# Decode attention over two KV caches: K and V in rows of 160 tokens, five heads to a group, in place of rows of 128 tokens and two heads

## The chip, the cores and the metric

One NeuronCore of a Trainium2 chip runs the whole program. The metric is the device time of one execution in microseconds (us). Engines are named as in the profile: PE (TensorE), PEld (its weight loads), DVE (VectorE), ACT (ScalarE), POOL (GpSimd), SP (SyncE, which issues nearly all transfers). The sequencer of an engine is the part that branches, computes addresses, waits for semaphores and hands instructions on; its own steps carry a `q` in the profile (PEldq, SPq).

## The reference

Two independent blocks A and B are computed and their outputs laid side by side. Each is one decode step of attention with batch 2, 32 heads, one query token and a cache of 8192 tokens, head size 192, model width 640, all bf16:

```python
q = (x @ wq).reshape(B, 1, 32, 192).transpose(0, 2, 1, 3)
scores = jnp.einsum("bhqd,bhkd->bhqk", q, k_cache) * (192 ** -0.5)
p = softmax(scores, axis=-1)
o = jnp.einsum("bhqk,bhkd->bhqd", p, v_cache)
return o.transpose(0, 2, 1, 3).reshape(B, 1, 32 * 192) @ wo
```

K and V of both blocks are 805 MB; with wq and wo it is 837 MB, each byte read once.

## The kernel before, in words

**Units.** Seen flat, a cache is 2 x 32 heads of 8192 tokens of 192 numbers. One load takes two heads as 128 rows of 128 tokens (`T = 128`, 49152 B a row): partitions 0 to 63 hold the first head, 64 to 127 the second. There are 32 such units to a block, 64 in all (`NP`); each has one load of K and one of V (6144 KB each).

**Ring.** `rings` has three slots of 61440 B a partition. K and V loads go round them: a load may be issued when the load two before it has landed (`ks`, `vs`) and when the slot's last user is done (`pv` for V's matmuls, `su` for the scores' matmuls). This is written out in `next_k` and `next_v` on SP. The same slots hold wq at the start and wo at the end.

**One unit.** The loop over `t` on each engine:

- PE, `make_q` (L322): one matmul with a selector spreads the two heads' queries over the partitions in PSUM; ACT (L272, L273) copies them to `qt`.
- DVE (L241): K is multiplied in place by the query, in four pieces of 32 tokens (128 x 6144 elements each).
- PE (L370): the 192 products of a token are added up in part: 12 matmuls with the identity add 16-wide pieces into `scps` (one PSUM bank for a piece of 32 tokens). The loop over `h` makes two turns of 24 matmuls.
- DVE (L246): reduces the last 16 to one score; L250 and L251 take each partition's maximum; POOL (L191) takes it over partitions; ACT (L296) scales it.
- ACT (L302): exp with the sum of each row (`rs`) into `pb`.
- PE (L385): PV. 64 matmuls of 384 columns, two tokens each, in four turns of a loop over `g` with 16 matmuls (`PG = 16`). Every turn tests the semaphore `vh`.
- `closing` on DVE and `gather` on ACT add the two halves and divide by the row sum; `put` on PE (L327) places the result in `oall`, four matmuls a unit.

PE's order in turn `t` of its loop (from L356) is: `make_q(t + 1)`, scores of unit `t`, `put`, PV of unit `t - 1`. So the scores of a unit stand ahead of the PV of the unit before.

**Ends.** At the start PE multiplies x by wq of both blocks (L411, six turns of ten matmuls a block) as wq lands. At the end wo of block A, the last V in two halves, and wo of block B in pieces (`PIECES`) are loaded; `rows` (L339) multiplies by wo.

Of the kernel before, what the change touches and what calls it, by code (L numbers as in the profile page):

```python
# [5 lines left out]
ALU = mybir.AluOpType  # L6
# [3 lines left out]
F32 = mybir.dt.float32  # L10
def build_kernel(nc, blocks, out):
# [5 lines left out]
    PB = Hn // 2  # L17
    UB = B * PB
    NP = NBLK * UB
    T = 128  # L20
    TQ = T // 4
    QW = TQ * Dh
# [4 lines left out]
    RW = T * Dh  # L27
    SW = DC * N
    QC = 512
    NQP = N // (2 * QC)  # L30
    NH2 = D // 2
    WR = N // 128
    PW = 34
    PG = 16
    PQ = T // 2 // PG
    CUTS = [48]
    PIECES = [24, 15, 6, 2, 1]

    with ExitStack() as es:
# [4 lines left out]
        sc = sb("sc", [128, T], F32)  # L44
        qt = sb("qt", [128, Dh], BF16)
        mp = sb("mp", [128, 2], F32)
        mg = sb("mg", [128, 2], F32)
        nb = sb("nb", [128, 1], F32)
        rs = sb("rs", [128, PW], F32)
        rc = sb("rc", [2, 1], F32)  # L50
        oodd = sb("oodd", [2, Dh], F32)
        on = sb("on", [2, Dh], BF16)
        xr = sb("xr", [4, D], BF16)
        xT = sb("xT", [128, DC, 4], BF16)
        ident = sb("ident", [128, 128], BF16)
        place = sb("place", [2, 264], BF16)
        ones = sb("ones", [128, 1], F32)
        oallS = sb("oallS", [128, WR, B], BF16)
        actd = sb("actd", [128, 2], F32)
        warm = sb("warm", [128, 2], F32)  # L60
        sb("pad", [128, 1648], BF16)
        rings = sb("rings", [128, 3 * SW], BF16)
        qrow = sb("qrow", [36, N], BF16)
        pb = sb("pb", [128, T // 2, PW], BF16)
        sel = sb("sel", [36, NBLK * B, 128], BF16)
        out_sb = [sb(f"out_sb{k}", [PW, NH2], BF16) for k in range(NBLK)]
# [4 lines left out]
        oall = ps("oall", [128, 2, 512], F32)  # L71
        outps = qps
        scflat = scps[:].rearrange("p k n -> p (k n)")
        oflat = oall[:].rearrange("p k n -> p (k n)")

        Z = {n: sem(n) for n in ("held", "wq", "wq0", "wq1", "xs", "k0", "ks", "vs", "vh", "os", "init", "dv", "xp", "xt",
                                 "pr", "qe", "qk", "qtd", "mu", "su", "re", "mx", "ar", "nbd", "ex", "pv", "od", "dd", "on",
                                 "pl", "oa", "ca", "oe", "wa0")}
# [7 lines left out]
        def flat(name, blk):  # L86
            return blocks[blk][name].rearrange("b h s d -> (b h s d)").rearrange("(u f) -> u f", f=RW)

        def k_slot(eng, t):
            return eng.snap(((t * 2 + 2 - ((t + (NP - 1)) >> 6)) % 3) * SW)  # L90

        def program_sync(eng):
# [5 lines left out]
            def load(name, blk, row, at, sem):  # L98
                src = flat(name, blk)
                src = src[row:row + 128, :] if isinstance(row, int) else src[bass.ds(row, 128), :]  # L100
                dst = rings[:, at:at + RW] if isinstance(at, int) else rings[:, bass.ds(at, RW)]
                eng.dma_start(dst, src).then_inc(Z[sem], 16)  # L102

            load("k", 0, 0, 2 * SW, "k0")
            eng.wait_ge(Z["pr"], NQP)
            load("k", 0, 128, 0, "ks")
            eng.wait_ge(Z["pr"], 2 * NQP)
            load("v", 0, 0, SW, "vs")
            eng.wait_ge(Z["su"], 2)

            def next_k(u, row, blk, at, wait_k, wait_p):
                hold(eng, "ks", wait_k)
                hold(eng, "pv", wait_p)
                load("k", blk, row, at, "ks")

            def next_v(u, row, blk, at, wait_v, wait_s):
                hold(eng, "vs", wait_v)
                hold(eng, "su", wait_s)
                load("v", blk, row, at, "vs")

            def step(t, u0, blk_v, blk_k):
                if isinstance(t, int):
                    u = u0
                    next_k(u, (u + 1) % UB * 128, blk_k, ((2 * u + 3) % 3) * SW, 16 * u + 16, PQ * (u + 1))
                    next_v(u, u % UB * 128, blk_v, ((2 * u + 4) % 3) * SW, 16 * u, 2 * u + 2)
                else:
                    u = eng.snap(t + u0)
                    r = eng.snap((u * 2) % 3)
                    rk, rv = eng.snap(t * 128 + (u0 + 1) % UB * 128), eng.snap(t * 128 + u0 % UB * 128)
                    next_k(u, rk, blk_k, eng.snap(r * SW), eng.snap(u * 16 + 16), eng.snap(u * PQ + PQ))  # L130
                    next_v(u, rv, blk_v, eng.snap(((r + 1) % 3) * SW), eng.snap(u * 16), eng.snap(u * 2 + 2))

            with eng.Fori(0, UB - 2) as t:
                step(t, 1, 0, 0)
            step(0, UB - 1, 0, 1)
            with eng.Fori(0, UB - 1) as t:
                step(t, UB, 1, 1)
            eng.wait_ge(Z["pv"], PQ * NP)
            for blk in range(NBLK):
                w = blocks[blk]["wo"].rearrange("(p r) n -> p (r n)", r=WR)  # L140
                if not blk:
                    r0 = 0
                    for k, n in enumerate(CUTS):
                        eng.dma_start(rings[:, r0 * D:(r0 + n) * D], w[:, r0 * D:(r0 + n) * D]).then_inc(Z[f"wa{k}"], 16)
                        r0 += n
                    eng.wait_ge(Z["su"], 2 * NP)
                    src = flat("v", 1)[(UB - 1) * 128:UB * 128, :]
                    for g in range(2):
                        a, e = g * RW // 2, (g + 1) * RW // 2
                        eng.dma_start(rings[:, SW + a:SW + e], src[:, a:e]).then_inc(vq[g], 16)  # L150
                else:
                    r0 = 0
                    for k, n in enumerate(PIECES):
                        eng.wait_ge(Z["ca"], k + 1)
                        eng.dma_start(rings[:, r0 * D:(r0 + n) * D], w[:, r0 * D:(r0 + n) * D]).then_inc(ws[k], 16)
                        r0 += n
# [8 lines left out]
        def program_pool(eng):  # L165
            eng.memset(warm[:], 0.0).then_inc(Z["init"], 1)
            eng.wait_ge(Z["init"], 1)
            eng.partition_all_reduce(warm[:, 1:2], warm[:, 0:1], 128, bass.bass_isa.ReduceOp.max)
            eng.memset(ident[:], 1.0).then_inc(Z["init"], 1)
            eng.wait_ge(Z["init"], 2)  # L170
            eng.affine_select(out=ident[:], in_=ident[:], compare_op=ALU.is_equal, fill=0.0, base=0,
                              pattern=[[-1, 128]], channel_multiplier=1).then_inc(Z["init"], 1)
            eng.memset(sel[:], 1.0).then_inc(Z["init"], 1)
            eng.wait_ge(Z["init"], 4)
            for k in range(NBLK * B):
                eng.affine_select(out=sel[:, k, :], in_=sel[:, k, :], compare_op=ALU.is_equal, fill=0.0,
                                  base=-(34 * (k // B) + k % B), pattern=[[0, 128]], channel_multiplier=1)
            eng.memset(place[:], 1.0).then_inc(Z["init"], 1)
            eng.wait_ge(Z["init"], 5)
            eng.affine_select(out=place[:], in_=place[:], compare_op=ALU.is_equal, fill=0.0, base=-128,  # L180
                              pattern=[[1, 264]], channel_multiplier=-4)
            eng.memset(ones[:], 1.0)
            eng.memset(rs[:], 0.0)
            eng.memset(pb[:], 0.0)
            eng.memset(mp[:], -3.0e38).then_inc(Z["init"], 1)
# [3 lines left out]
            with eng.Fori(0, NP) as t:  # L189
                hold(eng, "mx", eng.snap(t + 1))  # L190
                eng.partition_all_reduce(mg[:], mp[:], 128, bass.bass_isa.ReduceOp.max).then_inc(Z["ar"], 1)  # L191
            k = 0
            for i, n in enumerate(CUTS):
                eng.wait_ge(Z[f"wa{i}"], 16)
                while k < len(PIECES) and sum(PIECES[:k + 1]) <= sum(CUTS[:i + 1]):
                    eng.sem_inc(ws[k], 16)
                    k += 1
            eng.wait_ge(vq[0], 16)
            eng.sem_inc(Z["vs"], 16)
            eng.wait_ge(vq[1], 16)  # L200
            eng.sem_inc(Z["vh"], 2)

        def spread(eng, blk):
            eng.wait_ge(Z["pl"], (blk + 1) * UB + 3)
            dst = oallS[:].rearrange("p r b -> p b r")
            src = oall[:, 1 - blk, :].rearrange("p (b r) -> p b r", b=B)[:, ::-1, 0:WR]
            return eng.activation(dst, src, ACTF.Identity) if blk else eng.tensor_copy(dst, src)

        INIT = 6

        def program_vector(eng):
            eng.memset(qrow[:], 0.0).then_inc(Z["dv"], 1)  # L212
            eng.memset(on[:], 0.0)
            eng.memset(oodd[:], 0.0)
            eng.memset(ops[0:PW, 0:2 * Dh], 0.0)
            eng.memset(oall[:], 0.0)
            eng.memset(ops[0:2, 448:449], 1.0).then_inc(Z["dv"], 1)
            eng.sem_inc(Z["on"], 1)
# [3 lines left out]
            def closing(c):  # L222
                eng.wait_ge(Z["pv"], PQ * c if isinstance(c, int) else eng.snap(c * PQ))
                eng.reciprocal(rc[:], ops[0:2, 448:449]).then_inc(Z["dd"], 1)  # L224
                eng.wait_ge(Z["od"], c)
# [31 lines left out]
        def program_scalar(eng):  # L257
# [17 lines left out]
            for blk in range(NBLK):  # L275
# [4 lines left out]
                if not blk:  # L280
                    eng.wait_ge(Z["qk"], 1)
                    make_qt()
# [198 lines left out]
```

## Time and profile before

| what | value |
|---|---|
| median of 3 runs | 1935.44 us (1935.39 to 1935.62) |
| profiled execution, first to last instruction (span) | 1934.3 us |
| busy share PE / PEld / DVE / ACT / POOL | 81% / 38% / 56% / 10% / 1% |
| moved by DMA | 836.78 MB, 433 GB/s over the span |
| mean granted PE clock | 0.965 of full speed |

The profiled execution has no time of its own beside its span; the runs are 1.1 us longer than it. How to read the rows that follow: a row of groups gives line, engine, operation, output and input with their shapes and the count, then busy time and mean ns of one, then how long the engine stood idle before them and what ended that. A row of the timeline gives start, length, engine, line, operation, count, and in brackets the idle time before it with what ended it; "issue" there means that nothing but the engine's own sequencer was waited for. A row of windows gives for a stretch the busy time and number of instructions on PE, PEld, DVE, ACT and POOL, then the granted clock, the DMA engines' busy share and GB/s.

### The profile page before, as it was taken

How to read it: one execution, taken by the hardware profiler on the slowest of the kernel's cores; microseconds unless marked ns; L12 is line 12 of the kernel's file. 1: busy time of each engine (PE TensorE's matmuls, PEld its weight loads, DVE VectorE, ACT ScalarE, POOL GpSimd, SP SyncE). 2: the span in 40 equal slices, each digit the busy share in tenths (PEclk: the TensorE clock that was granted, in tenths of full speed). 3: DMA queues.
4: the chain of work that ended last, by engine and by line, in shares of the span. 5: the costliest groups of instructions: out<-in, count | busy, mean ns of one | idle time of the engine just before them, and what ended most of it. 6: DMA issues, size and time to landing. Idle time of an engine off the chain costs nothing.

```text
span 1934.3 us, 31141 instructions
## 1 busy us (share of the span) xinstructions
PE 1558.2 (81%) x7939; PEld 743.0 (38%) x7939; DVE 1075.6 (56%) x717; ACT 186.5 (10%) x598; POOL 27.9 (1%) x83
## 2 busy tenths in 40 slices
PE   5787888887888887888887888887888888888887
PEld 1343333333333333333333333333433333433434
DVE  0665565565565565565565565565565565565560
ACT  2110010010010010010010010010010010010010
POOL 1000000000000000000000000000000000000000
PEclk9899999999999999999999999999999999999999
DMA  9999999999999999999999999999999999999999
GB/s 421 425 439 439 423 439 439 425 437 439 430 432 439 431 431 439 433 429 439 435 427 439 437 425 439 437 425 439 437 425 439 439 425 437 439 430 432 439 435 394
DMA packets 19896, 836.78 MB, mean 433 GB/s; under 512 B 2220, under 2 KB 2360, under 8 KB 2744
## 3 DMA queue, kind: packets, MB, share of 16 engines
q1 hardware_dynamic: 19880, 836.78, 100.0%
q10 hardware_dynamic: 16, 0.01, 0.0%
HBM read 836.77 MB, written 0.01 MB: 433 GB/s over the span
## 4 chain that ended last, share of the span: by engine, by line
DMA 44%; PE 32%; DVE 10%; issue 10%; another core or an unknown queue 2%; DVEq 1%; SPq 0%; ACT 0%; POOLq 0%
DMA rings<-in_B_k_cache_dram 22%; DMA rings<-in_A_k_cache_dram 19%; PE ops L385 18%; PE scps L370 12%; DVE rings L241 10%; DMA rings<-in_A_wo_dram 2%; DMA rings<-in_B_wo_dram 1%; DVEq L241 1%; PE oall L327 0%; PE qps L339 0%; PE ops L379 0%; SPq L102 0%; DVE qrow L212 0%; DVE sc L246 0%
## 5 line engine op out<-in xcount | busy, mean ns | idle before, releaser
L241 DVE TENSOR_TENSOR rings<-rings,qt 128x6144 bf16 x256 | 842.5, 3353 | 722.9 <-DMA rings<-in_B_k_cache_dram 351.0
L385 PE MATMUL ops<-rings,pb 128*34 x4096 | 712.9, 327 | 166.9 <-issue 166.9
L370 PE MATMUL scps<-rings,ident 128*128 x3072 | 749.0, 403 | 105.5 <-DVE rings L241 102.6
L385 PEld LDWEIGHTS ops<-rings,pb 128*34 x4096 | 381.3, 93 | 483.0 <-issue 233.5
L370 PEld LDWEIGHTS scps<-rings,ident 128*128 128x128 bf16 x3072 | 314.5, 102 | 524.0 <-issue 249.6
L246 DVE TENSOR_REDUCE sc<-scps 128x64 f32<-128x1024 f32 x128 | 155.5, 1215 | 81.4 <-PE scps L370 81.4
L286 ACT ACTIVATE oodd<-ops 2x192 f32<-2x192 f32 x65 | 20.9, 321 | 731.4 <-PE ops L385 731.4
L272 ACT ACTIVATE qt<-qps 64x192 bf16<-64x192 f32 x65 | 21.0, 323 | 650.1 <-DVE rings L241 649.6
L302 ACT ACTIVATE pb<-sc,nb 64x128 bf16<-64x128 f32 x128 | 82.4, 644 | 2.6
L322 PE MATMUL qps<-qrow,sel 36*128 (+1 forms) x66 | 21.8, 331 | 72.4 <-issue 69.6
L296 ACT ACTIVATE nb<-mg 64x1 f32<-64x1 f32 x128 | 25.7, 201 | 302.8 <-POOL mg L191 302.1
L191 POOL PARTITION_ALL_REDUCE mg<-mp x64 | 22.7, 354 | 1856.8 <-DVE mp L251 1856.8
L322 PEld LDWEIGHTS qps<-qrow,sel 36*128 (+1 forms) x66 | 6.1, 93 | 94.0 <-issue 94.0
L302 ACT ACTIVATION_READ_ACCUMULATOR pb<-sc,nb 64x1 f32 x128 | 39.2, 306 | 0.0
L411 PE MATMUL scps<-rings,xT 128*4 x120 | 29.4, 410 | 6.3 <-POOLq L188 6.3
L224 DVE RECIPROCAL rc<-ops 2x1 f32<-2x1 f32 x66 | 9.8, 149 | 34.5 <-PE ops L385 34.5
L327 PEld LDWEIGHTS oall<-on,place 2*128 x260 | 12.5, 92 | 29.7 <-issue 29.2
L226 DVE TENSOR_TENSOR oodd<-ops,oodd 2x192 f32<-2x192 f32 x66 | 21.5, 326 | 0.4 <-ACT oodd L286 0.4
L229 DVE TENSOR_SCALAR on<-oodd,rc 2x192 bf16<-2x192 f32 x66 | 20.3, 307 | 2.3
L273 ACT ACTIVATE qt<-qps 64x192 bf16<-64x192 f32 x65 | 21.1, 325 | 0.8
L327 PE MATMUL oall<-on,place 2*128 2x48 bf16 x260 | 19.6, 183 | 1.9 <-DVE on L229 1.7
L411 PEld LDWEIGHTS scps<-rings,xT 128*4 128x4 bf16 x120 | 10.7, 89 | 24.2 <-issue 12.2
(38 smaller groups left out, 109.9 us busy)
## 6 DMA issues: line engine op xcount, KB each, us to landing
rings<-in_A_k_cache_dram SPq DMA_DIRECT2D x32, 6144.0 KB, 26.8
rings<-in_A_v_cache_dram SPq DMA_DIRECT2D x32, 6144.0 KB, 26.5
rings<-in_B_k_cache_dram SPq DMA_DIRECT2D x32, 6144.0 KB, 26.7
rings<-in_B_v_cache_dram SPq DMA_DIRECT2D x31, 6144.0 KB, 26.6
rings<-in_B_wq_dram SPq DMA_DIRECT2D x1, 7680.0 KB, 37.9
rings<-in_A_wo_dram SPq DMA_DIRECT2D x1, 7680.0 KB, 30.7
rings<-in_A_wq_dram SPq DMA_DIRECT2D x1, 7296.0 KB, 20.2
rings<-in_B_v_cache_dram SPq DMA_DIRECT2D x2, 3072.0 KB, 26.8
```

The lines of the kernel that those rows point to most:

```text
L191: eng.partition_all_reduce(mg[:], mp[:], 128, bass.bass_isa.ReduceOp.max).then_inc(Z["ar"], 1)
L226: eng.tensor_tensor(oodd[:], ops[0:2, 0:Dh], oodd[:], ALU.add).then_inc(Z["dd"], 1)
L241: eng.tensor_tensor(k3, k3, q3, ALU.mult).then_inc(Z["mu"], 1)
L246: eng.tensor_reduce(sc[:, h * 2 * TQ:(h + 1) * 2 * TQ], scps[:, 2 * h:2 * h + 2, :].rearrange("p k (t g) -> p (k t) g", g=DG), AXL.X, ALU. ...
L273: eng.activation(qt[64:128, :], qps[64:128, Dh:2 * Dh], ACTF.Identity).then_inc(Z["qtd"], 1)
L296: ins = eng.activation(nb[p0:p0 + 64, :], mg[p0:p0 + 64, h:h + 1], ACTF.Identity, scale=-scale)
L302: ins = eng.activation(pb[p0:p0 + 64, :, h::32], sc[p0:p0 + 64, :].rearrange("p (j a) -> p j a", a=2), ACTF.Exp, bias=nb[p0:p0 + 64, :], s ...
L322: eng.matmul(qps[:, 0:2 * Dh], sel[:].rearrange("p s m -> p (s m)")[:, bass.ds(k, 128)], qrow[:, bass.ds(c, 2 * Dh)], start=True, stop=Tru ...
L327: ins = eng.matmul(oflat[:, bass.ds(sec, WR)], place[:, bass.ds(at - a, 128)], on[:, a * WR:(a + 1) * WR], start=False, stop=False, skip_g ...
L370: ins = eng.matmul(dst, ident[:], src[:, :, 0:DG], start=(j == 0), stop=(j == NJ - 1))
L385: ins = eng.matmul(ops[0:PW, 0:2 * Dh], pbflat[:, bass.ds(aj + j * PW, PW)], rings[:, bass.ds(vj + j * (2 * Dh), 2 * Dh)], start=False, st ...
L411: ins = eng.matmul(scflat[0:4, bass.ds(to + h * QC, QC)], xT[:, c, :], rings[:, bass.ds(at + (c * N + h * QC), QC)], start=(c == 0), stop= ...
```

## The change

Rows become 160 tokens (five chunks of 32, 61440 B a partition), so that one load fills a whole slot (7680 KB). 8192 is no multiple of 160: two loads of 128 rows hold five heads (40960 tokens), and a partition can hold the end of one head and the start of the next. Which chunk of a partition belongs to which of the five heads is told by masks: `MK` spreads the right query over each partition (six matmuls, for up to three different queries of a load), `MN` adds -1e38 to the maxima and biases of chunks that aren't the head's, so that their exponentials are zero. A block is 12 groups of five heads and one group of four heads with rows of 128 tokens (`kind(t)`); there are 26 groups (`NG`).

- SP: four loads a group through the same three slots, in the order K_a, K_b, V_a, V_b, two semaphores (`la`, `lb`) in turn. The last V_b comes in pieces of three chunks and one.
- PE: order in turn `t` is `queries(t)`, `put`, PV of group `t - 1` (both V loads), scores of group `t` (both K loads). PV has 80 matmuls a load in ten turns of eight (`PG = 8`); `queries` has a loop of five matmuls, a copy by ACT and six matmuls into `scps`; `put` has eight matmuls; scores run in turns of 12 matmuls.
- DVE: five multiplies of K_a, one of K_b, reduction of K_a's scores, four multiplies of K_b, closing, reduction of K_b's scores, then maxima by chunk, masks, maxima by head and biases.
- ACT: copies of the queries, then 18 exponentials a group (three spans of a row by three heads, for each load).
- POOL: builds the masks at the start, and between two maxima passes on the landing of both V loads (`vs`).
- Start: the queries of a block come in twelve turns of five matmuls, and all of them ahead of the first group.

The diff, cut to the lines that run in the loops:

```diff
-        T = 128
+        TC = 32; CW = TC * Dh; NCH = 5; SCH = 4; T = NCH * TC; NS = 5
-        PG = 16
-        PQ = T // 2 // PG
+        PG = 8
+        LATE = 3
+        SPANS = [[(0, 1), (1, 2), (2, 5)], [(0, 3), (3, 4), (4, 5)]]
-        scps = ps("scps", [128, 4, 512], F32)
+        scps = ps("scps", [128, NCH, 512], F32)
...
 # SP
+            def step(g, row, blk, nch, unit):
+                hold(eng, "la", val(g * 32))
+                hold(eng, "su", val(g * (2 * NCH)))
+                load("k", blk, row, nch, s0, "la")
+                hold(eng, "lb", val(g * 32))
+                hold(eng, "pv", val(g * 2 + 1))
+                load("k", blk, row1, nch, s1, "lb")
+                if not isinstance(g, int) or g < NG - 1:
+                    hold(eng, "la", val(g * 32 + 16))
+                    hold(eng, "pv", val(g * 2 + 2))
+                    load("v", blk, row, nch, s2, "la")
+                    hold(eng, "lb", val(g * 32 + 16))
+                    hold(eng, "su", val(g * (2 * NCH) + NCH))
+                    load("v", blk, row1, nch, s0, "lb")
...
 # POOL
+            with eng.Fori(0, NG - 1) as t:
+                maximum(eng.snap(t + 1))
+                landed = eng.snap(t * 32 + 32)
+                for name in ("la", "lb"):
+                    eng.wait_ge(Z[name], landed)
+                    eng.sem_inc(Z["vs"], 1)
...
 # DVE
+                for c in range(NCH):
+                    multiply(at[0], 0, c)
+                eng.wait_ge(Z["lb"], landed)
+                multiply(at[1], 1, 0)
+                eng.wait_ge(Z["ex"], eng.snap(t * 2 + 1))
+                reduce(0, eng.snap(t * (2 * NCH) + NCH))
+                for c in range(1, NCH):
+                    multiply(at[1], 1, c)
+                closing(t - 1)
...
+                eng.tensor_scalar(last, last, flag[:, bass.ds(w, 1)], None, ALU.min).then_inc(Z["ch"], 1)
+                reduce(1, eng.snap(t * (2 * NCH) + 2 * NCH))
...
+                eng.tensor_reduce(cm, sc[:].rearrange("p u (c t) -> p (u c) t", t=TC), AXL.X,
+                                  ALU.max).then_inc(Z["ch"], 1)
...
+                eng.tensor_reduce(mp, nb[:], AXL.X, ALU.max).then_inc(Z["mx"], 1)
+                eng.wait_ge(Z["ar"], eng.snap(t + 1))
+                eng.scalar_tensor_tensor(nb[:], mg.unsqueeze(2).broadcast_to([128, NS, 2 * NCH]), -scale, mask,
+                                         ALU.mult, ALU.add).then_inc(Z["nbd"], 1)
...
 # ACT
+            def queries(n):
+                eng.wait_ge(Z["qx"], n * NS if isinstance(n, int) else eng.snap(n * NS))
+                eng.activation(qh[:], qps[0:NS, 0:Dh], ACTF.Identity).then_inc(Z["qh"], 1)
+                eng.wait_ge(Z["qk"], n)
+                eng.activation(qt[:].rearrange("p u v d -> p (u v d)").rearrange("p (k n) -> p k n", k=3),
+                               scps[:, 0:3, 0:2 * Dh], ACTF.Identity).then_inc(Z["qtd"], 1)
+            def exps(n):
+                eng.wait_ge(Z["nbd"], n)
+                for u in range(2):
+                    for v, (c0, c1) in enumerate(SPANS[u]):
+                        src = sc[:, u, c0 * TC:c1 * TC].rearrange("p (b i a) -> p b i a", i=4, a=2)
+                        for s in range(2 * u, 2 * u + 3):
+                            dst = pb[:, u, 4 * c0:4 * c1, :, :, s].rearrange("p b a i -> p b i a")
+                            k = u * NCH + 2 * u + v
+                            ins = eng.activation(dst, src, ACTF.Exp, bias=nb[:, s, k:k + 1], scale=scale,
+                                                 accum_out=rs[:, u, v, s:s + 1])
+                    ins.then_inc(Z["ex"], 1)
+            with eng.Fori(0, NG - 1) as t:
+                queries(eng.snap(t + 2))
+                exps(eng.snap(t + 1))
+                gather(t)
...
 # PE
+            def queries(t):
+                n = eng.snap(t * NS + 128 - ((t + 19) >> 5))
+                eng.wait_ge(Z["re"], eng.snap(t * 2 + 1))
+                blank(qps[0:NS, 500:501], NS, True)
+                with eng.Fori(0, NS) as m:
+                    h = eng.snap(n + m)
+                    eng.matmul(qps[0:NS, 0:Dh], emf[:, bass.ds(eng.snap(((h >> 5) & 3) * (NS * NS) + m * NS), NS)],
+                               qrow[:, bass.ds(eng.snap((h & 31) * Dh), Dh)], start=False, stop=False,
+                               skip_group_check=True).then_inc(Z["qx"], 1)
+                eng.wait_ge(Z["qh"], eng.snap(t + 1))
+                for k in range(6):
+                    ins = eng.matmul(scps[:, k // 2, (k % 2) * Dh:(k % 2 + 1) * Dh],
+                                     mkf[:, bass.ds(eng.snap(w * (6 + k // 3 - k) + k * 128), 128)],
+                                     qh[:], start=True, stop=True)
...
+                            with eng.Fori(0, 2) as u:
+                                hold(eng, "ex", w)
+                                hold(eng, "vs", w)
+                                with eng.Fori(0, n2) as g:
+                                    eng.wait_ge(Z["vh"], eng.snap(((g + 2) >> 3) * lu + 1))
+                                    aj, vj = eng.snap(g * (PG * 16) + pat), eng.snap(g * (PG * 2 * Dh) + v_at)
+                                    for j in range(PG):
+                                        eng.matmul(ops[0:PW, 0:2 * Dh],
+                                                   pbflat[:, bass.ds(aj + (j // 4 * 64 + j % 4 * 8), PW)],
+                                                   rings[:, bass.ds(vj + j * (2 * Dh), 2 * Dh)], start=False, stop=False,
+                                                   skip_group_check=True)
+                                blank(ops[0:PW, 500:501], PW, False).then_inc(Z["pv"], 1)
...
+                        with eng.Fori(0, 2) as u:
+                            hold(eng, "re", eng.snap(t * 2 + u + 1))
+                            with eng.Fori(0, NCH) as c:
+                                eng.wait_ge(Z["mu"], eng.snap(n + c))
+                                for j in range(NJ):
+                                    ins = eng.matmul(dst, ident[:], ringt[:, bass.ds(at, TC), j * DG:(j + 1) * DG],
+                                                     start=(j == 0), stop=(j == NJ - 1))
+                                ins.then_inc(Z["su"], 1)
```

More of the change, by code (lines that the diff above doesn't have):

```diff
@@ L178, in program_pool @@
[L178 to L182, printed above, removed]
+                only(Em[:, k], ALU.is_equal, 0.0, -(34 * (k // B) + k % B), [[0, NS], [0, NS]], 1)
+            for tile, pat in kinds:
+                only(tile, ALU.is_ge, 0.0, 0, pat, -HCH)
```

463 lines of the change are left out of this document (237 added, 226 removed).

## The prediction

> **What bounds the kernel now.** I read the page first: engine shares, the span in 40 slices, then the kinds of DMA traffic. Then the table by stage for the long middle of the run, and only after that the order of time inside one unit.
>
> ```profile
> span 1934.3 us, 31141 instructions
> PE 1558.2 (81%) x7939; PEld 743.0 (38%) x7939; DVE 1075.6 (56%) x717; ACT 186.5 (10%) x598; POOL 27.9 (1%) x83
> DMA  9999999999999999999999999999999999999999
> 200.00:1800.00 1600.00, 1302.97 (x6574) 622.91 (x6571) 920.95 (x609) 146.87 (x497) 19.83 (x56) 0.97 1.00 434
> 910.10 13.17 DVE L241 TENSOR_TENSOR rings<-rings,qt 128x6144 bf16 x4 [10.84 <-DMA rings<-in_A_k_cache_dram]
> 939.12 13.16 DVE L241 TENSOR_TENSOR rings<-rings,qt 128x6144 bf16 x4 [11.05 <-DMA rings<-in_A_k_cache_dram]
> ```
>
> The DMA engines are full in every slice; the row of windows gives share 1.00 and 434 GB/s for 1600 us on end. Each K multiply on VectorE starts when its K has landed (it stood idle 11 us for that), and those starts are 29.0 us apart: 12.58 MB of K and V at 434 GB/s. So transfers set the pace. But TensorE is busy 81%, and that is the number to watch. How close is it? Right after the start the kernel had two loads in hand and TensorE did not have to wait; there one whole unit of two heads can be timed.
>
> ```profile
> 101.17 2.82 PE L385 MATMUL ops<-rings,pb 128*34 x16 [0.66 <-issue]
> 105.08 0.33 PE L322 MATMUL qps<-qrow,sel 36*128 x1 [1.08 <-issue]
> 105.98 10.53 PE L370 MATMUL scps<-rings,ident 128*128 x48 [0.57 <-issue]
> 116.73 5.36 PE L385 MATMUL ops<-rings,pb 128*34 x32
> 122.75 2.78 PE L385 MATMUL ops<-rings,pb 128*34 x16 [0.66 <-issue]
> 126.20 2.81 PE L385 MATMUL ops<-rings,pb 128*34 x16 [0.67 <-issue]
> 130.12 0.33 PE L322 MATMUL qps<-qrow,sel 36*128 x1 [1.11 <-issue]
> ```
>
> From one query matmul (105.08) to the next (130.12) TensorE needs 25.0 us with nothing to wait for, against 29.0 us of transfers. So the margin is only 4 us in 29. Note also the idle 0.66 to 0.67 us before each 16 PV matmuls, ended by "issue": that is a turn of the loop over `g`, in which TensorE's own sequencer branches, computes addresses and tests a semaphore. One turn of 16 takes 126.20 - 122.75 = 3.45 us.
>
> **The change, part by part.** *The loads.* Five heads are 31.46 MB in four loads; at 434 GB/s that is 72.5 us. Do rows of 61440 B go faster? The nearest transfer of that shape is wo of block A, 7680 KB:
>
> ```profile
> 1854.58 0.34 SPq L102 DMA_DIRECT2D rings<-in_B_v_cache_dram  x1
> 1868.53 0.36 SPq L144 DMA_DIRECT2D rings<-in_A_wo_dram  x1
> rings<-in_B_v_cache_dram SPq DMA_DIRECT2D x31, 6144.0 KB, 26.6
> rings<-in_A_wo_dram SPq DMA_DIRECT2D x1, 7680.0 KB, 30.7
> ```
>
> The V before it lands at 1854.58 + 26.6 = 1881.2, wo at 1868.53 + 30.7 = 1899.2: 18.05 us, where 7.86 MB at 434 GB/s are 18.12. So 96 large loads gain 7 us at most and perhaps nothing. I take -2 us, and it counts only while transfers are the bound.
>
> *The order on TensorE.* Per group of five heads its stream is: queries, `put`, all PV of the group before, then the scores of both K loads. Its PV waits for the exponentials of that group, everything behind it (scores) waits with it, and VectorE cannot go beyond the first chunk of the second K before it has reduced the first K's scores, since the five PSUM banks of `scps` serve both. So the group is a ring; I walk round it from the end of a group's second reduction. The rows for the terms:
>
> ```profile
> 15.52 0.19 PE L400 MATMUL qps<-ident,xr 4*128 4x4 bf16 x1 [0.34 <-issue]
> 16.05 0.19 PE L400 MATMUL qps<-ident,xr 4*128 4x4 bf16 x1 [0.34 <-issue]
> 38.43 0.33 PE L322 MATMUL qps<-qrow,sel 36*128 36x384 bf16 x1 [1.37 <-ACT qrow L278]
> 38.80 0.32 ACT L272 ACTIVATE qt<-qps 64x192 bf16<-64x192 f32 x1 [0.50 <-PE qps L322]
> 37.28 1.01 ACT L278 ACTIVATE qrow<-scps  x1 [1.15 <-PE scps L411]
> 911.93 0.65 ACT L302 ACTIVATE pb<-sc,nb 64x128 bf16<-64x128 f32 x1
> 912.60 0.64 ACT L302 ACTIVATE pb<-sc,nb 64x128 bf16<-64x128 f32 x1
> L246 DVE TENSOR_REDUCE sc<-scps 128x64 f32<-128x1024 f32 x128 | 155.5, 1215 | 81.4 <-PE scps L370 81.4
> L382 PEldq ALU_OP  x512: 42/42/43, 90.2 to 1917.7; - x171
> L381 PEldq COMPARE_BRANCH  x256: 82/227/228, 93.3 to 1920.6; - x128
> ```
>
> 1. Queries: a loop of one matmul takes 16.05 - 15.52 = 0.53 us a turn with one address. The new turn computes a head number, a mask offset and a row offset; make_q's gap of 1.11 us bounds it above. I take 1.0 x 5. Then a copy on ScalarE (0.32), two hand-overs (0.37 each, 38.43 to 38.80) and six matmuls with two addresses (0.15 each): 7.0 us. Bounds 5 and 10.
> 2. ScalarE copies qt, 1152 columns: from 192 in 0.32 and 1024 in 1.01, 1.2 us. Only then, being in order, it starts the exponentials, although bias and maximum (six small VectorE and GpSimd steps) are long done: they lie beside 1 (bare, they would cost some 2 us). The first nine pairs: a pair of 128 columns is 0.67 us start to start, by the same slope 0.59 for 32 columns and 0.64 for 96: 5.5 us, plus 0.3 for the last to end. Sum 14.0. `put` (eight matmuls) lies beside it on TensorE and costs nothing; without that cover it would cost about 3.
> 3. PV. The turn now holds 8 matmuls, not 16. Matmuls of that line are 0.163 apart (5.36 less the last one's 0.33, over 31), so a turn is 3.45 - 8 x 0.163 = 2.15; the piece index is now an add, a shift, a multiply and an add where it was an and and an add, and sequencer operations of 42 ns come about 0.1 apart by the gaps above: 2.35 us, bounds 2.05 and 2.7. There are 10 turns for each of two V loads: 47.0, against 2.5 x 4 x 3.45 = 34.5 before for the same tokens. Heads of the loops 1.9 (estimate from the 1.11 gap), row sums 0.5. Sum 63.4.
> 4. Scores of the first K: 12 matmuls in 10.53 / 4 = 2.63, five chunks 13.2, head 1.2. VectorE multiplied them during 3. Sum 77.8.
> 5. Reduction on VectorE: 1215 ns for 1024 columns, 2.9 for 2560. Sum 80.7.
> 6. Four multiplies of the second K, 13.2 (the x4 row above). The chunk before the reduction is already done. Sum 93.9.
> 7. The last chunk's scores behind the last multiply, 2.63 and 0.45 of hand-over: 97.0. The closing's three VectorE steps lie beside it.
> 8. Second reduction 2.9: 99.9, say 100 us a group, against 72.5 of transfers.
>
> So the loads wait for room, no longer the engines for loads. K_b waits on SP for V_a's PV, V_a for V_b's, and each is queued behind the one before; in a ring of 100 us each still lands before it is read: V_b, the last, is issued when the first K's scores are done (77.8), behind V_a (63.4), and lands near 102, 2 us into the next round. GpSimd now waits for both V loads ahead of its next maximum; that one is due 98 us later, so the wait costs nothing (in a ring at the transfers' pace it would still have some 50). DMA share would be about 72%.
>
> *The ends.* Up to the first R: queries of both blocks end near 56, plus 2 for twelve short turns in place of six; then queries 8.2, six multiplies 19.8, reduction, four multiplies, last chunk, reduction: 58 + 8.2 + 19.8 + 2.9 + 13.2 + 3.1 + 2.9 = 108. Longer POOL set-up is covered by the first wq (multiplication by it starts at 22).
>
> ```profile
> 54.97 1.01 ACT L278 ACTIVATE qrow<-scps  x1 [1.19 <-PE scps L411]
> 22.15 14.91 PE L411 MATMUL scps<-rings,xT 128*4 x60 [4.80 <-POOLq L188]
> 1899.37 6.68 PE L339 MATMUL qps<-rings,oallS 128*2 128x320 bf16 x96 [1.81 <-POOLq L196]
> 1918.15 2.77 PE L385 MATMUL ops<-rings,pb 128*34 x16 [0.69 <-issue]
> 1923.73 8.72 PE L339 MATMUL qps<-rings,oallS 128*2 128x320 bf16 x96 [0.55 <-ACT oallS L207]
> ```
>
> After the last R: block A's output rows 6.7 with 2.3 ahead, put and head 4.5, 16 turns of PV (4-chunk rows) 37.6 and a head 1.6, closing to rows 2.8 (1920.92 to 1923.73) plus 3 for the longer put, rows 6.7, end 1.9 (1932.45 to 1934.3): 67. The uneven pieces of the last V decide nothing, for V has landed by then.
>
> *Sum.* 26 groups, 25 full turns of the ring; one holds the small group's PV, four turns less: 108 + 25 x 100 - 9 + 67 = 2666 us of span. The runs lie 1.1 over the profiled span (1935.44 to 1934.3), so 2667.
>
> [...] The rows say 227 ns for most of these branches. [...]
>
> **The rivals.** *A, the loop turns are partly hidden.* At 116.73 there are 32 matmuls in 5.36 us without the gap at the turn: the sequencer had run ahead during the scores, where a matmul takes 0.22 us. If PV's turns were all hidden like that, PV is 160 x 0.163 = 26, the ring 79, the time about 2667 - 25 x 21 - 16 x 1.05 = 2125. Against it: from 122.75 on the gaps are back, and the new PV starts after a semaphore wait with no lead. A part of it, say 2300, is thinkable. [...]
>
> *B, not slower.* The whole overhead of TensorE's sequencer vanishes (queries 7 to 2, PV 47 to 26, heads 4 to 0): the ring becomes 70, under 72.5, transfers stay the bound, and the time is 1935 less the 2 us for larger rows: 1933. The point from which it decides is a ring of 72.5, so less than 2.5 us of sequencer time may stay of 30. Against it stand all the rows with "issue".
>
> *C, slower yet: a lower clock.*
>
> ```profile
> 943.12 12.22 PE L370 MATMUL scps<-rings,ident 128*128 x48 [1.15 <-DVE rings L241]
> 70.00:80.00 10.00, 4.07 (x14) 1.45 (x12) 8.30 (x6) 2.02 (x7) 0.36 (x1) 0.68 0.93 403
> ```
>
> After idle stretches the granted clock falls (0.68 here) and 48 score matmuls take 12.22, not 10.53. The new ring has more idle stretches. At half clock throughout, a chunk costs 2.6 more on six chunks and PV about 10: a ring of 126. Half of that is 113, and 2990 us. The drops here are short, so little of it.
>
> **How the numbers follow.** The likeliest is the ring of 100 us: 0.80, 2667 us. Its own bounds: PV's turn -6 to +7 us a group, queries -2 to +3, exponentials 0.5 either way: -8.5 to +10.5, times 25: 2450 to 2930; the upper end needs all at once, so 2870. A has 0.10 (2125 to 2450), C 0.06, B 0.04. Two in ten are left out at 2450 to 2870. The measurement tells 0.2% from no change: slower 0.96; B halved into same 0.02 and faster 0.02.
>
> **What would show it.** Right: DMA's slices at 7 in place of 9; TensorE's busy share down with much "issue" before the PV matmuls; VectorE idle ended by the scores, not by K's landing; reductions 100 us apart; the chain through PV, ScalarE's exponentials and VectorE's multiplies. Wrong: VectorE's K multiply still ended by DMA (B), PV matmuls in one run without gaps (A), a granted clock under 0.9 (C). The prediction fails in size if the PV turn is not 2.35 or the query loop not 1.0 us.

## The result, and the profile after

The changed kernel takes 2562.61 us (median of 5 runs, 2560.2 to 2565.49); the kernel before took 1935.53 beside it. The ratio is 1.3238, 95% interval 1.3222 to 1.3255. The forecast was 2667 us, in a range of 2450 to 2870.

The page of the changed kernel: span, engine shares and the DMA row of the 40 slices; then a row of windows over 2000 us (columns as before: PE, PEld, DVE, ACT, POOL busy, granted clock, DMA share, GB/s); then the costliest groups.

```profile
span 2564.2 us, 33482 instructions
PE 1713.5 (67%) x8451; PEld 810.9 (32%) x8451; DVE 1057.5 (41%) x529; ACT 222.3 (9%) x1046; POOL 20.8 (1%) x64
DMA  9967967967967967966786886886886786786784
300.00:2300.00 2000.00, 1345.16 (x6581) 639.38 (x6579) 849.43 (x416) 165.37 (x819) 7.72 (x21) 0.89 0.77 327
L476 PE MATMUL ops<-rings,pb 128*37 x4096 | 807.1, 343 | 427.0 <-issue 426.5
L298 DVE TENSOR_REDUCE sc<-scps 128x160 f32<-128x2560 f32 x52 | 146.9, 2825 | 395.5 <-PE scps L495 395.5
```

The transfers now stand still for about a quarter of the time (share 0.77, 327 GB/s in place of 1.00 and 434). No engine is full either: TensorE's share fell from 81% to 67%. That is what a ring looks like: each step waits for the one before it. Two rows name steps. The PV matmuls have 427 us of idle time ahead of them, put down to "issue", TensorE's own sequencer; before it was 166.9. And VectorE's reductions wait 395 us for the scores.

One round of the ring, from the timeline (`...` stands for turns, matmuls and exponentials left out; rows of engines that only work beside the ring are left out too):

```profile
1179.88 8.30 PE L476 MATMUL ops<-rings,pb 128*37 x32 [2.82 <-issue]
1188.97 1.49 PE L476 MATMUL ops<-rings,pb 128*37 x8 [0.79 <-issue]
1191.23 1.51 PE L476 MATMUL ops<-rings,pb 128*37 x8 [0.77 <-issue]
...
1225.52 0.44 PE L482 MATMUL ops<-small,rs 128*5 128x1 f32 x12
1226.88 13.12 PE L495 MATMUL scps<-rings,ident 128*128 x60 [0.93 <-issue]
1240.04 2.82 DVE L298 TENSOR_REDUCE sc<-scps 128x160 f32<-128x2560 f32 x1 [17.14 <-PE scps L495]
1242.78 13.15 DVE L294 TENSOR_TENSOR rings<-rings,qt 128x6144 bf16 x4
1243.78 12.15 PE L495 MATMUL scps<-rings,ident 128*128 x48 [3.78 <-DVE sc L298]
1256.39 2.76 PE L495 MATMUL scps<-rings,ident 128*128 x12 [0.46 <-DVE rings L294]
1259.19 2.83 DVE L298 TENSOR_REDUCE sc<-scps 128x160 f32<-128x2560 f32 x1 [2.34 <-PE scps L495]
1262.97 0.24 PE L407 MATMUL qps<-qrow,Em 128*5 x1 [0.73 <-issue]
1264.20 0.32 PE L407 MATMUL qps<-qrow,Em 128*5 x1 [0.99 <-issue]
...
1268.78 1.13 PE L414 MATMUL scps<-qh,MK 5*128 5x192 bf16 x6 [0.69 <-ACT qh L358]
1269.95 1.13 ACT L360 ACTIVATE qt<-scps 128x1152 bf16<-128x1152 f32 x1 [1.50 <-PE scps L414]
1270.98 0.43 ACT L375 ACTIVATE pb<-sc,nb 128x32 bf16<-128x32 f32 x1
1271.28 0.43 ACT L375 ACTIVATE pb<-sc,nb 128x32 bf16<-128x32 f32 x1
...
1273.52 0.88 ACT L375 ACTIVATE pb<-sc,nb 128x96 bf16<-128x96 f32 x1
1275.61 8.31 PE L476 MATMUL ops<-rings,pb 128*37 x32 [2.84 <-issue]
```

PV starts at 1179.88 and again at 1275.61: a round is 95.7 us, where four loads need 72.5. Each row begins within a microsecond or so of the end of the one above it (or of the work that `...` stands for). Only the 48 score matmuls at 1243.78 lie beside another row: they follow VectorE's four multiplies chunk by chunk.

### The profile page after: what moved, and what is told of

It is laid out like the page before. It is cut to its first block, busy times and chain, and to the rows that moved or that the text cites. A ratio compares the mean times of both kernels' runs of the same rounds, so it can differ in the third digit from the quotient of the medians.

```text
span 2564.2 us, 33482 instructions
## 1 busy us (share of the span) xinstructions
PE 1713.5 (67%) x8451; PEld 810.9 (32%) x8451; DVE 1057.5 (41%) x529; ACT 222.3 (9%) x1046; POOL 20.8 (1%) x64
## 3 DMA queue, kind: packets, MB, share of 16 engines
q1 hardware_dynamic: 16424, 836.77, 76.8%
## 4 chain that ended last, share of the span: by engine, by line
PE 53%; issue 18%; DMA 15%; DVE 10%; ACT 4%; SPq 0%; DVEq 0%; POOL 0%; ACTq 0%; POOLq 0%
PE scps L495 26%; PE ops L476 22%; DMA rings<-in_B_k_cache_dram 7%; DMA rings<-in_A_k_cache_dram 6%; DVE sc L298 5%; DVE rings L294 5%; ACT pb L375 3%; PE qps L407 2%; DMA rings<-in_B_wq_dram 1%; PE scps L414 1%; PE qps L438 1%; PE scps L520 1%; ACT qh L358 0%; PE ops L482 0%; PE qps L398 0%
## 5 line engine op out<-in xcount | busy, mean ns | idle before, releaser
L294 DVE TENSOR_TENSOR rings<-rings,qt 128x6144 bf16 x260 | 856.5, 3353 | 1023.7 <-DMA rings<-in_B_k_cache_dram 495.3
L476 PE MATMUL ops<-rings,pb 128*37 x4096 | 807.1, 343 | 427.0 <-issue 426.5
L476 PEld LDWEIGHTS ops<-rings,pb 128*37 x4096 | 409.5, 100 | 814.5 <-issue 596.0
L298 DVE TENSOR_REDUCE sc<-scps 128x160 f32<-128x2560 f32 x52 | 146.9, 2825 | 395.5 <-PE scps L495 395.5
L375 ACT ACTIVATE pb<-sc,nb 128x32 bf16<-128x32 f32 (+1 forms) x468 | 161.4, 583 | 37.7 <-DVE nb L333 37.7
L375 ACT ACTIVATION_READ_ACCUMULATOR pb<-sc,nb 128x1 f32 x468 | 132.1, 322 | 0.0
L407 PE MATMUL qps<-qrow,Em 128*5 x130 | 40.4, 311 | 112.3 <-issue 112.3
L426 PE MATMUL oall<-on,place 5*128 5x48 bf16 x216 | 33.4, 213 | 27.4 <-issue 25.6
L414 PE MATMUL scps<-qh,MK 5*128 5x192 bf16 x156 | 29.6, 348 | 18.1 <-ACT qh L358 18.1
L426 PEld LDWEIGHTS oall<-on,place 5*128 x216 | 21.5, 100 | 44.9 <-issue 39.2
L360 ACT ACTIVATE qt<-scps 128x1152 bf16<-128x1152 f32 x26 | 29.4, 1130 | 39.4 <-PE scps L414 39.4
L398 PEld LDWEIGHTS qps<-ident 128*5 128x5 bf16 x26 | 2.1, 81 | 87.6 <-DVE sc L298 85.3
## 6 DMA issues: line engine op xcount, KB each, us to landing
rings<-in_A_k_cache_dram SPq DMA_DIRECT2D x2, 6144.0 KB, 18.6
```

The costliest lines, as they stand in the source:

```text
L294: eng.tensor_tensor(k3, k3, q3, ALU.mult).then_inc(Z["mu"], 1)
L298: eng.tensor_reduce(sc[:, u, :], scps[:].rearrange("p k (t g) -> p (k t) g", g=DG), AXL.X, ALU.add).then_inc(Z["re"], 1)
L360: eng.activation(qt[:].rearrange("p u v d -> p (u v d)").rearrange("p (k n) -> p k n", k=3), scps[:, 0:3, 0:2 * Dh], ACTF.Identity).then_i ...
L375: ins = eng.activation(dst, src, ACTF.Exp, bias=nb[:, s, k:k + 1], scale=scale, accum_out=rs[:, u, v, s:s + 1])
L407: eng.matmul(qps[0:NS, 0:Dh], emf[:, bass.ds(eng.snap(((h >> 5) & 3) * (NS * NS) + m * NS), NS)], qrow[:, bass.ds(eng.snap((h & 31) * Dh), ...
L414: ins = eng.matmul(scps[:, k // 2, (k % 2) * Dh:(k % 2 + 1) * Dh], mkf[:, bass.ds(eng.snap(w * (6 + k // 3 - k) + k * 128), 128)], qh[:], ...
```

## The experiments

Theory S is the prediction's: the rounds are set by the ring, and most of what was added to it is loop turns of TensorE's sequencer. Against it stand L (the loads themselves have become slow), H (the lower granted clock) and, for single steps, P (only PV's turns count). The ring's length is read from the first and last start of the maxima by chunk (one a group, 25 rounds between them). It is a mean, and one of the 25 rounds holds a smaller group: in the changed kernel that round took 87.1 us and the others 95.6 to 95.7.

| kernel | time, us | one round, us |
|---|---|---|
| changed | 2562.6 | 95.4 |
| PV turns of 16 | 2307.7 | 85.3 |
| PV turns of 4 | 3086.2 | 115.5 |
| queries written out | 2497.3 | 92.8 |
| second K early | 2560.1 | 94.9 |
| PV written out | 2093.8 | 76.8 |
| PV and queries written out, second K early | 2311.3 | 85.1 |
| PV and queries written out | 2033.0 | 74.4 |
| the same, reductions split | 1975.1 | 72.2 |

**The size of a PV turn, both ways.** First twice as many matmuls to a turn:

```diff
-    PG = 8
+    PG = 16
...
-    eng.wait_ge(Z["vh"], eng.snap(((g + 2) >> 3) * lu + 1))
+    eng.wait_ge(Z["vh"], eng.snap(((g + 1) >> 2) * lu + 1))
```

> The changed kernel with 16 PV matmuls in a turn of the loop (five turns a load) and nothing else. Theory S (TensorE's sequencer: the turns of its loops lie on the ring of a group): a turn of 8 took 2.26 us, one of 16 then takes 2.26 + 8 x 0.163 = 3.56; a group saves 20 x 2.26 - 10 x 3.56 = 9.6 us, 24 big and two small groups 246 us: about 2317 us (2290 to 2345). Theory L (the loads: rows of 61440 B, or at most two loads in flight in a ring of three slots, are slower by themselves): no change, 2563. Theory H (the lower granted clock, 0.89 for 0.96, makes every matmul slower): no change beyond 1%.

Measured 2307.67 us (ratio to the kernel before 1.192, 1.1902 to 1.1938), 255 us less than the changed kernel. Then half as many, the same edit with `PG = 4`:

> The changed kernel with 4 PV matmuls in a turn (twenty turns a load). S: a turn takes 2.26 - 4 x 0.163 = 1.61, a group 40 x 1.61 = 64.4 in place of 45.2, all groups +492: about 3054 us (3000 to 3110). L and H: no change, 2563.

Measured 3086.19 us (1.5942, 1.5917 to 1.5966), 524 us more. The matmuls and the loads are the same in the three kernels; the round goes 85.3, 95.4, 115.5 us for 10, 20 and 40 turns. That is 1.01 us for each turn, from both steps. L and H are out as causes of these differences: both foretold none, and the granted clock was 0.88 in both runs (0.89 in the changed kernel). Of the 627 us by which the changed kernel is slower than the one before, 255 go when a turn holds 16 matmuls again, as it did before. What the branch, the address computation and the semaphore test each add to a turn is not separated here.

**The loads alone.** What do rows of 61440 B cost or bring once the engines are out of the way? One turn of PV a load in place of ten:

```diff
-    with eng.Fori(0, n2) as g:
-        eng.wait_ge(Z["vh"], eng.snap(((g + 2) >> 3) * lu + 1))
+    with eng.Fori(0, 1) as g:
+        eng.wait_ge(Z["vh"], eng.snap(lu + 1))
```

> The changed kernel with one turn of PV (8 matmuls) a load; the other nine turns, nine tenths of PV, are left out. All loads stay, with their rows, order and waits. S: the ring loses 18 x 2.26 = 41 us and becomes some 55, under the 72.5 of transfers, so transfers set the pace again at the rate of before: 1933 us (1925 to 1945). L: the loads stay slow whatever the engines do, and the time stays well over 2000.

Measured 1939.29 us (1.002, 1.0011 to 1.0029). Its windows, and the starts of two groups' first chunk of the second K:

```profile
300.00:1800.00 1500.00, 839.74 (x3566) 364.02 (x3567) 843.00 (x420) 165.50 (x819) 7.72 (x21) 0.73 1.00 434
1007.74 3.36 DVE L294 TENSOR_TENSOR rings<-rings,qt 128x6144 bf16 x1 [1.65 <-DMA rings<-in_B_k_cache_dram]
1080.21 3.36 DVE L294 TENSOR_TENSOR rings<-rings,qt 128x6144 bf16 x1 [1.65 <-DMA rings<-in_B_k_cache_dram]
```

Share 1.00 and 434 GB/s, as before the change, and 72.47 us for four loads, where 2.5 units of 29.0 are 72.5. The moments at which loads land in the two traces say it more finely: 18.118 us apart for the large rows (mean of 90, without the start and the small groups), 14.500 for the small ones (mean of 126), and 1.25 x 14.500 is 18.125. The longer rows gain 0.007 us a load, less than 1 us in the whole run. Most of the 4 us over the kernel before come from the start: the third, fourth and fifth gap between landings of K and V are 18.8, 19.8 and 19.1 us there. L is out altogether, and so is any hope that came from the row length.

**The turn in the kernel before.** If a turn of the loop costs TensorE a microsecond, the old kernel must pay as well once its margin of 4 us a unit is gone. `PG = 4`, with `late` and the last increment of `vh` scaled:

> The kernel before with 4 PV matmuls in a turn of its loop in place of 16 (16 turns a unit), its loads of 128-token rows untouched. S: a turn of 16 took 3.45, one of 4 takes 3.45 - 12 x 0.163 = 1.5, a unit 16 x 1.5 = 24.0 in place of 13.8; without waits a unit took 25.0 and then takes 35.2, over the 29.0 of transfers: 64 x 35.2 + 75 for the ends = 2330 us (2270 to 2390). L: 1935, for the loads are those of before.

Measured 2455.17 us (1.2669, 1.2642 to 1.2695): slower with its loads untouched, as S says, but 125 us over the expected time. The timeline shows the two terms that were too small:

```profile
1229.65 0.33 PE L322 MATMUL qps<-qrow,sel 36*128 x1 [1.14 <-issue]
1230.58 12.22 PE L370 MATMUL scps<-rings,ident 128*128 x48 [0.60 <-issue]
1243.02 2.22 PE L385 MATMUL ops<-rings,pb 128*34 x12
1245.96 0.85 PE L385 MATMUL ops<-rings,pb 128*34 x4 [0.73 <-issue]
1247.55 0.82 PE L385 MATMUL ops<-rings,pb 128*34 x4 [0.74 <-issue]
1266.92 0.33 PE L322 MATMUL qps<-qrow,sel 36*128 x1 [1.17 <-issue]
```

A turn of 4 is 1.59 us, not 1.5 (16 of them: 1.4 us), and the scores take 12.22, not 10.53. A unit is 37.3 us in place of 35.2, less than the two terms say together: the first three turns, right behind the scores, ran without gaps and took 2.9 us and not 4.8 (1243.02 to 1245.96), a lead of which the unit that the forecast went by had 0.9 us. With `PG = 8` the margin should be just used up:

> The kernel before with 8 PV matmuls in a turn (eight turns a unit). S: a turn is 1.585 (measured with 4) + 4 x 0.163 = 2.24, a unit without waits 25.0 - 4 x 3.45 + 8 x 2.24 = 29.1, and up to 1.7 more where the scores start at a lower clock, against 29.0 of transfers: the margin of 4 us is just used up, 1942 to 2050 us. L: 1935.5, no change.

Measured 1958.0 us (1.0109, 1.0093 to 1.0124), 22 us slower, inside the range: a turn was 2.2 us and a unit 29.6. And with the loop written out, so that TensorE has less to do than before:

```diff
-    with eng.Fori(0, PQ) as g:
-        eng.wait_ge(Z["vh"], eng.snap((g & late) + 1))
+    for g in range(PQ):
+        if g in (0, PQ // 2):
+            eng.wait_ge(Z["vh"], eng.snap(late + 1) if g else 1)
```

> The kernel before with its 64 PV matmuls of a unit written out, no loop, so TensorE has some 2.5 us a unit less to do. S: transfers are the bound there, no change: 1935.5 us within 2. A theory in which the loop's turns cost time wherever they stand: 64 x 2.6 = 166 us less.

Measured 1936.82 us (1.0007, 0.9998 to 1.0016): no change. The 64 matmuls ran in one piece, and the time saved turned into waiting for VectorE, which waits for K:

```profile
928.43 10.56 PE L386 MATMUL ops<-rings,pb 128*34 x64
944.26 12.11 PE L370 MATMUL scps<-rings,ident 128*128 x48 [5.00 <-DVE rings L241]
```

The same turns cost nothing where a margin covers them and 1.0 us each where they are on the ring.

**The queries' loop.**

```diff
-    with eng.Fori(0, NS) as m:
+    for m in range(NS):
```

> The changed kernel with the loop of five query matmuls written out; PV's turns of 8 as they are. S: a turn took 1.2 us, of which about 0.45 is loop (branch and counter); five are 2.2 us a group shorter, and all that follows them on the ring (copy, exponentials, PV) comes that much sooner: 2563 - 25 x 2.2 = 2508 us (2490 to 2525). Rival P (only PV's turns are on the ring, the queries lie beside the exponentials): no change.

Measured 2497.34 us (1.2896, 1.2876 to 1.2915), 65 us less; the round lost 2.6 us. P is out: the queries are on the ring too.

**VectorE's order.** All chunks of the second K multiplied ahead of the first reduction:

```diff
-    multiply(at[1], 1, 0)
+    for c in range(NCH):
+        multiply(at[1], 1, c)
     eng.wait_ge(Z["ex"], eng.snap(t * 2 + 1))
     reduce(0, eng.snap(t * (2 * NCH) + NCH))
-    for c in range(1, NCH):
-        multiply(at[1], 1, c)
```

> The changed kernel with VectorE multiplying all five chunks of the second K before it reduces the first K's scores (in place of one before and four after). S: VectorE stands on the ring between the two sets of scores; the second set then follows at TensorE's pace, 13.7 us from the first reduction in place of 16.3: 2563 - 25 x 2.6 = 2498 us (2480 to 2515). Rival P: no change, VectorE is off the path (41% busy).

Measured 2560.14 us (1.3219, 1.3198 to 1.3239): no gain to speak of, as P foretold, but not for P's reason. VectorE's multiplies did leave the ring, and TensorE gave most of the time back. Timeline and windows of that kernel:

```profile
1246.55 2.83 DVE L298 TENSOR_REDUCE sc<-scps 128x160 f32<-128x2560 f32 x1 [3.38 <-PE scps L494]
1250.30 14.81 PE L494 MATMUL scps<-rings,ident 128*128 x60 [3.78 <-DVE sc L298]
1251.55:1254.96 3.41, 3.41 (x9) 1.21 (x8) 0.00 (x0) 0.00 (x0) 0.00 (x0) 0.50 1.07 461
1250.30:1254.00 3.70, 3.70 (x12) 1.57 (x13) 0.00 (x0) 0.00 (x0) 0.00 (x0) 0.67 0.99 425
```

TensorE idles 3.78 us through the reduction; then the granted clock is 0.67 over the next 3.7 us (0.50 from 1251.55 to 1254.96), and 60 matmuls take 14.81 where the first set took 13.12. In the changed kernel the same 3.78 us of idle time (1243.78 in the round above) cost nothing, since the multiplies paced the matmuls anyway. So the round lost 0.5 us only, and the 12 us of 25 rounds went at the start: the first maxima came at 127.9 us in place of 113.7, for in the first group nothing covers the four multiplies, and the second scores no longer run beside them.

**PV written out, and the edits together.** The diff is as in the kernel before; groups of four heads run the fifth chunk too, against zeros.

> The changed kernel with the 80 PV matmuls of a load written out, no loop; the groups of four heads run 80 too. S: PV of a group goes from 46.1 us to 160 x 0.163 and about 3.5 for heads and a slow start, 29.6: the ring is 16.5 shorter (9 for the two small groups): 2563 - 23 x 16.5 - 2 x 9 = 2165 us (2130 to 2200). L: no change; a part of the turns would then not be on the ring.

Measured 2093.81 us (1.0814, 1.0797 to 1.083), under the range of 2130 to 2200: the round lost 18.6 us and not 16.5. The heads went with the loops: the first scores now begin right behind the row sums (1232.92 + 0.44 to 1233.32), where the changed kernel idles 0.93 us there. Then all three edits:

> The three edits together: PV written out, queries written out, second K multiplied early. S: the terms add, ring 95.7 - 16.5 - 2.2 - 2.6 = 74.4 us, still over 72.5 of transfers: 1939 (the time with a tenth of PV) + 25 x 1.9 = 1987 us (1940 to 2030). Rival P: about the time of PV written out alone, 2165.

Measured 2311.34 us (1.1936, 1.192 to 1.1952): 218 us *slower* than PV written out alone. A miss; the terms don't add. Timeline of the three edits together, and last a piece of the chain that the page follows back:

```profile
1271.77 13.12 PE L494 MATMUL scps<-rings,ident 128*128 x60
1280.19 16.43 DVE L294 TENSOR_TENSOR rings<-rings,qt 128x6144 bf16 x5 [11.94 <-DMA rings<-in_B_k_cache_dram]
1296.54 2.82 DVE L298 TENSOR_REDUCE sc<-scps 128x160 f32<-128x2560 f32 x1
1258.82 21.17 DMA rings<-in_B_k_cache_dram
```

The first scores were done at 1284.9, but VectorE was inside five multiplies of a second K that had landed only at about 1280, and reduced at 1296.5: 11.7 us lost in this round. The chain runs through that load. That K is issued when V_a's PV is done. In the changed kernel it landed 20.5 us ahead of the first reduction (1219.54 to 1240.04), here 4.7 us ahead of the end of the first scores, so work put ahead of the reduction drags its landing onto the ring. If so, leaving that edit out brings the gains back:

> The changed kernel with PV and queries written out, and VectorE's order left as the change has it (one chunk of the second K before the first reduction). S with the finding that the early second K made the first reduction wait for that K's landing: without it the two gains add, 2094 - 65 = 2029 us (2010 to 2045). If the early K was not what cost 217 us in the three edits together, this one stays near 2300.

Measured 2033.01 us (1.0499, 1.0483 to 1.0515), as expected: the early K was the cause. One more step, the reductions split:

```diff
-    eng.wait_ge(Z["su"], upto)
-    eng.tensor_reduce(sc[:, u, :], scps[:]...)
+    eng.wait_ge(Z["su"], upto - 1)
+    eng.tensor_reduce(sc[:, u, 0:SCH * TC], scps[:, 0:SCH, :]...)
+    eng.wait_ge(Z["su"], upto)
+    eng.tensor_reduce(sc[:, u, SCH * TC:T], scps[:, SCH:NCH, :]...)
```

> As the run before, and each reduction of scores in two: four chunks while TensorE still adds the fifth, then the fifth. S: the ring is 77.4 (PV written out) - 2.6 (queries) - 1.6 and 2.1 (reductions, by the rows of the run with PV written out) = 71.1, under 72.5, so transfers come back as the bound: 1940 to 1985 us, the lower end if the loads' own waits for room don't add. Nothing in it can be faster than 1935, for a load of rows of 61440 B lands 18.117 us after the one before it, where 1.25 loads of rows of 49152 B take 18.125.

Measured 1975.12 us (1.0201, 1.0187 to 1.0215). Its windows in the middle, in two gaps and at the end:

```profile
300.00:1800.00 1500.00, 1264.46 (x6519) 650.27 (x6518) 837.48 (x458) 165.18 (x818) 7.76 (x21) 0.89 1.00 432
132.70:138.00 5.30, 5.30 (x35) 3.25 (x34) 4.91 (x2) 0.00 (x0) 0.00 (x0) 1.00 0.00 0
997.00:1002.70 5.70, 5.70 (x38) 3.52 (x36) 5.44 (x2) 0.00 (x0) 0.00 (x0) 1.00 0.00 0
1954.00:1972.00 18.00, 12.81 (x131) 7.23 (x129) 0.81 (x3) 1.03 (x3) 0.00 (x0) 0.81 0.00 0
```

The middle is back at the transfers' pace. What is left over the kernel with a tenth of PV (36 us) lies mostly outside the rounds: 18 us without any transfer at the close, for PV of the last group and the output rows come after the last byte, and two gaps between loads, over 5 us each, at the start and where the blocks change. Some 6 us are left without an account. No version of the change got under the kernel before. No run alters TensorE's order by itself (the kernel before has a unit's scores ahead of the PV of the unit before), so what that order costs is not measured on its own.

## Why the prediction was right

By its own steps, in us from the end of the second reduction (the first two rows from 1262.0, the end of the round shown above; the others from 1166.3, its beginning):

| step | forecast | measured |
|---|---|---|
| queries done | 7.0 | 7.9 |
| first nine exponentials done | 14.0 | 12.4 |
| PV and row sums done | 63.4 | 59.7 |
| scores of the first K done | 77.8 | 73.7 |
| first reduction done | 80.7 | 76.6 |
| four multiplies done | 93.9 | 89.6 |
| last scores done | 97.0 | 92.9 |
| second reduction done | 99.9 | 95.7 |

- The bound moved as forecast: from transfers to a ring through TensorE, VectorE and ScalarE. The sum came out better than its terms: the start and the queries were too short, the exponentials and PV too long. The margin of 4 us in 29, read from one unit that had nothing to wait for, was the right number to look at; the kernel before with turns of 8 shows that it is real.
- The round was 4.2 us too long in the forecast: 25 rounds were to take 2491 us and took 2384. The start was 5.7 us too short (113.7 us to the first maxima, 108 forecast): the first multiply began at 72.0 and not at 66.2, for the queries of the two blocks ended at 61.6 (58 forecast) and the first group's took 10.4 (8.2). The end was right (66.5 behind the last maxima, 67 forecast). Together that is the miss of 102 us in the span, 2564.2 for 2666.
- The mis-sized terms. Exponentials: a pair of 32 columns was priced at 0.59 us by a line through longer ones; pairs start 0.30 apart (1270.98 to 1271.28), so nine with the end of the last take 3.4 and not 5.8. A query turn was 1.2 and not 1.0. A PV turn was 2.26 (1191.23 less 1188.97) and not 2.35. The scores of the first K with the way to them took 14.0 and not 14.4. Reductions and multiplies came out within 0.2.
- The effect of larger rows on the loads, taken as -2 us with a bound of 7, is under 1 us.
- The branches of the new PV loop have a median of 223 ns, those of the old one 227 (the prediction's row of L381): they kept their length, and the round was shorter than forecast through the exponentials and PV's turn.

```profile
L472 PEldq COMPARE_BRANCH  x512: 82/223/234, 128.4 to 2548.2; - x171
```

- What it had wrong beside the sizes. A K multiply of VectorE that waits for a landing was to be the sign of rival B, and it is there all the same: 15.41 us ahead of the first multiply of a round, 1023.7 us in the run. It lies beside PV and decides nothing. And the prediction says that VectorE cannot go beyond the second K's first chunk ahead of the reduction because of the PSUM banks. That was only the order of the program: with the second K early it multiplied all five chunks.

```profile
1183.62 16.43 DVE L294 TENSOR_TENSOR rings<-rings,qt 128x6144 bf16 x5 [15.41 <-DMA rings<-in_A_k_cache_dram]
L294 DVE TENSOR_TENSOR rings<-rings,qt 128x6144 bf16 x260 | 856.5, 3353 | 1023.7 <-DMA rings<-in_B_k_cache_dram 495.3
```

- Rival A (turns hidden) did not hold even where the gaps are gone. The first four turns of a round run in one piece of 8.30, but the fifth starts 9.09 us after the first (1179.88 to 1188.97), 2.27 for each turn, as for the others. The granted clock was 0.50 up to 1185.6, and eight matmuls took some 2.5 us there (18 in 5.72), longer than the usual turn of 2.26: the gaps were filled and no time was saved. Rival B (not slower) needed the sequencer's 30 us a round to vanish; with PV and the queries written out and the reductions split the round did reach the transfers' pace, and the time still stayed 2% over. Rival C (clock): it fell to 0.89, as feared, but in stretches where it costs little, below.

```profile
1179.88:1185.60 5.72, 5.72 (x18) 2.82 (x19) 1.98 (x1) 1.62 (x14) 0.00 (x0) 0.50 0.32 137
1166.30:1179.90 13.60, 4.13 (x22) 2.03 (x22) 1.11 (x4) 5.95 (x29) 0.37 (x1) 0.58 0.95 409
1179.90:1226.00 46.10, 32.73 (x174) 16.86 (x174) 19.79 (x6) 1.61 (x15) 0.00 (x0) 0.94 0.37 154
1226.00:1243.00 17.00, 13.12 (x60) 5.83 (x60) 2.96 (x2) 0.31 (x1) 0.00 (x0) 1.00 0.99 411
1243.00:1262.00 19.00, 14.91 (x60) 6.22 (x60) 16.62 (x9) 0.00 (x0) 0.00 (x0) 0.91 0.83 347
```

The clock is low (0.58) where TensorE has almost nothing to do and 0.91 to 1.00 where it works. The two stretches in which it works at a lower clock, the start of PV and the start of the second scores, are paced by the sequencer and by VectorE's multiplies.

## What to carry to other kernels

When transfers are the bound, time one unit in which nothing had to be waited for: the difference to the transfers' pace is all that a change may add to an engine's instruction stream. Here that was 4 us in 29, and each further turn of PV's loop made the round 1.01 us longer, for the same matmuls in turns of 16, 8 or 4. An order of work in which each step needs the one before it makes a ring of waits, in which terms add that used to lie beside each other; there, an edit that moves work earlier can pull a load's landing onto the path and cost more than it saves (with PV and the queries written out: 2311.3 us with the second K early, 2033.0 without). Longer rows gained nothing here: rows of 49152 B and rows of 61440 B both moved at 434 GB/s.

## What the runs showed of the hardware

- With the second K early, TensorE idled 3.78 us ahead of the second scores; the granted clock was then 0.50 over 3.41 us, and their 60 matmuls took 14.81 us where those of the first set took 13.12. In the changed kernel the same 3.78 us of idle time cost nothing, for there VectorE's four multiplies (13.15 us) set the pace of the scores.
- In the changed kernel an exponential of 32 columns with its row sum started 0.30 us after the one before; at 96 columns it was 0.36 to 0.44. These short activations were cheaper than a line through longer ones says (0.59 by the prediction's line).
